# Attention with a mixture of adapters: results stored two chunks at a time, key rows loaded from another queue

## The chip, the cores and the metric

The kernel runs on one core of a Trainium2 chip. The core has five engines with a queue each, which run their instructions in the order written: TensorE (PE in the profile; its weight loads are PEld), VectorE (DVE), ScalarE (ACT), GpSimd (POOL) and SyncE (SP), which only issues transfers. Transfers (DMAs) are issued from SP, ACT and POOL and are carried by 16 DMA engines. The metric is the device time of one execution in microseconds (us); lower is better.

## The reference

```
kv_pool = kv.reshape(B, H//4, 4, W//4, 4, C).mean(axis=(2, 4))      # 4 x 384 x 32 -> 768 keys a batch
k = v = kv_pool.reshape(B, -1, C) @ w_sr
a = softmax(q @ k.T / sqrt(C));  x = a @ v                          # 4 x 12288 queries, C = 128
logits = x @ w_gate                                                 # 8 experts, the two best count
w = softmax over the two best logits
out = x + sum over the two of  w * ((x @ A[e]) @ B[e])              # rank 16
```

Inputs and the output are float32. The output has 49152 rows of 128 values, 25.2 MB.

## The kernel before, in words

The queries are cut into 96 chunks of 512; a batch has 24, and four chunks are a group. The work of a chunk is spread over several "slots" of a loop over k, one slot a chunk:

- Scores (`scores`, L307): PE multiplies the transposed queries `qT` by the keys `kfT` into the PSUM tile `sg`; ACT takes the exponential into `em`. Three such units make a chunk.
- Values (`attend`): PE multiplies `em` with `vx` into `acc`. `vx` has the values, the router's logits and a column of ones for the sum.
- Normalizing (`normalize`, L328 and L336): DVE divides into `xn`, which holds the attention's result and the logits.
- Routing (`top`, `route`, `gates`, L356 to L384): DVE finds the best logits, POOL and ACT make the gates `gw`.
- Adapters: `xn` is transposed, multiplied by all the A (`down`, tile `h_ps`), gated by DVE (`gate`, L437), transposed again, and multiplied by all the B (`up`, tile `d_ps`).
- The end of a chunk (`finish`, L471): DVE adds `d_ps` and `xn` into a result tile `osb`, and SP stores it (`store`, L467).

The second transpose is done in one of three ways. Chunks of the list `by_queue` (from 9 to 65, three of every four) go through a DMA transpose from SP (`gate_turn`, L457, tiles `ht` and `t`), and their `up` comes six or seven slots later. Chunks of `by_strip` (66 to 89) have both transposes done by DMA, in one transfer from SP a slot (`turn_dma`, L423, tile `turn`), read two or three slots later. The other chunks are transposed by PE (tile `tt_ps`).

Chunks are therefore not finished in the order of their numbers: an entry of `by_queue` comes several slots after its neighbour.

The queries of a group are cast by a DMA of POOL into bfloat16 in memory (`cast_q`, L83) and brought back by a DMA transpose of SP (`load_qT`, L92). Those of the first two groups are loaded in float32 (`load_q`) and transposed by PE.

The keys of a batch come from three tiles `kvr` of 2 MB; the pool has three of them. Each is loaded in four parts of 512 KB (`load_kv`, L102): the first batch and the second from SP, the third and the fourth from ACT, one part every two slots, at the start of the slot (`begin`). Parts of the last two batches are asked for from slot 15 to slot 37 and from 39 to 61. POOL sums the parts (`add_patches`, L522), five slots after a part is asked for and later, and PE transposes the sums.

The order of all the work is written out by hand: `keep` fixes it on each engine. Result tiles rotate: a new tile takes the buffer of the eighth before it (`opool`, eight buffers of 256 KB) and waits until that one's store has landed. In the list of instructions every DMA of SP and ACT also takes the next of eight completion semaphores, and waits for the DMA that had it before.

The four last chunks have code of their own (`carry`, `add_here`, `add_there`), with stores of 256 KB.

Of the kernel before, what the change touches and what calls it, by code (L numbers as in the profile page):

```python
# [10 lines left out]
FP32 = mybir.dt.float32  # L11
# [4 lines left out]
ALU = mybir.AluOpType  # L16
# [4 lines left out]
def kernel(  # L21
# [10 lines left out]
    nc = tc.nc  # L32
    P = 128
    B, N, C = q.tensor.shape
# [4 lines left out]
    T = 512  # L39
    S = T // P  # L40
    GC = 4
    GT = GC * T
# [4 lines left out]
    NCHUNK = B * NB  # L47
# [10 lines left out]
    gpool = ctx.enter_context(tc.tile_pool(name="gpool", bufs=6))  # L58
    run = ctx.enter_context(tc.tile_pool(name="run", bufs=3))
    hpool = ctx.enter_context(tc.tile_pool(name="hpool", bufs=4))  # L60
    opool = ctx.enter_context(tc.tile_pool(name="opool", bufs=8))
    qdram = ctx.enter_context(tc.tile_pool(name="qdram", bufs=1, space=bass.MemoryType.DRAM))
    ps_s = ctx.enter_context(tc.tile_pool(name="ps_s", bufs=2, space=bass.MemoryType.PSUM))
    ps_a = ctx.enter_context(tc.tile_pool(name="ps_a", bufs=1, space=bass.MemoryType.PSUM))
# [2 lines left out]
    keep = tc.keep_in_program_order  # L67
# [9 lines left out]
    q_bf, qT, kvr, spare = {}, {}, {}, {}  # L77
# [17 lines left out]
    def load_kv(b, h, r, x):  # L95

        if (b, h) not in kvr:
            kvr[b, h] = kvpool.tile([P, 4, 2, 4 * C], FP32, tag="kvr", name="kvr")
        rows = H // 3
        src = kv[b, h * rows + r:(h + 1) * rows:4].rearrange("y (w k) c -> y w (k c)", k=8)  # L100
        if x is None:
            keep((nc.scalar if b > 1 else nc.sync).dma_start(kvr[b, h][:, r].rearrange("p g c -> p (g c)"), src))  # L102
        else:
            keep(nc.sync.dma_start(kvr[b, h][:, r, x], src[:, :, x * 4 * C:(x + 1) * 4 * C]))


    q_f = {}

    def load_q(g, m):
        if g:  # L110
            t = hpool.tile([P, 2, S, P], BF16, tag="ht", name="qf")
            q_f[g, m] = t.rearrange("p h s c -> p (h s c)").bitcast(FP32).rearrange("p (s c) -> p s c", s=S)
        else:
            q_f[g, m] = opool.tile([P, S, C], FP32, tag="osb", name="qf")
        src = q[0, g * GT:(g + 1) * GT].rearrange("(p j) c -> p j c", p=P)
        keep(nc.sync.dma_start(q_f[g, m], src[:, m * S:(m + 1) * S]))

# [37 lines left out]
    def load_first(h):  # L155
        for r in range(3):
            load_kv(0, h, r, None)
        for x in range(2):
            load_kv(0, h, 3, x)

    load_first(0)
    for m in range(GC):
        load_q(0, m)
    load_first(1)
    load_first(2)
    for m in range(GC):
        load_q(1, m)
# [118 lines left out]
    em, acc, xn, xg, srt, gw = {}, {}, {}, {}, {}, {}  # L286
    used = []
    tts, xT, hgT, hp, hg, dp = {}, {}, {}, {}, {}, {}
# [53 lines left out]
    SOLO, TURN = NCHUNK - 6, NCHUNK - 28  # L342
# [122 lines left out]
    def store(queue, k, osb, lo=0, hi=S):  # L465
        to = out[k // GC * GT:(k // GC + 1) * GT].rearrange("(p j) c -> p j c", p=P)
        keep(queue.dma_start(to[:, k % GC * S + lo:k % GC * S + hi], osb))  # L467

    def finish(k):
        osb = opool.tile([P, S, C], FP32, tag="osb", name="osb")  # L470
        keep(nc.vector.tensor_tensor(osb, dp[k], xn[k][:, :, 0:C], op=ALU.add))  # L471
        store(nc.sync, k, osb)
        for d in (em, acc, xn, xT, hgT, hp, hg, dp):
            d.pop(k, None)

# [30 lines left out]
    for b in range(2, B):  # L506
        for n in range(12):
            h, r, t = n // 4, n % 4, b * NB - 33 + 2 * n
# [15 lines left out]
    def begin(k):  # L524
        nonlocal sums, rest
        b, i = divmod(k, NB)
        g = k // GC
        if k in casts:
            cast_q(4 + casts.index(k))
        if k in halves:  # L530
            g, u = halves[k]
            cast_q(g, u, u + 4)
        if k in rows_at:
            load_kv(*rows_at[k], None)
        if i == 0 and 0 < b < B - 1:
            rest = prepare(b + 1, nc.gpsimd)[1]
        if k == 3:
            sums, rest = prepare(1, nc.gpsimd)
            sums = sum(sums, [])
        if 3 <= k < 15:  # L540
            load_kv(1, (k - 3) // 4, (k - 3) % 4, None)
        if k == 7:
            for _ in range(2):
                sums.pop(0)()
# [12 lines left out]
    enter, t, left = {}, 1, list(range(NCHUNK - 3))  # L557
# [6 lines left out]
    by_queue = [k for k in range(9, TURN - 2) if k % 4 != 2 and k != 10]  # L564
    by_strip = range(TURN - 2, SOLO)
    slot = {x_: t for t, xs in enter.items() for x_ in xs}
    taken = [slot[x_] + (3 if x_ in by_strip else 2) for x_ in slot if x_ not in by_queue]
    up_slot = {}
    for x_ in by_queue:
        t = slot[x_] + (7 if x_ < TURN - 12 else 6)  # L570
# [2 lines left out]
        taken.append(t)  # L573
        up_slot[x_] = t
    by_pe = enter[SOLO - 2][1:]
    assert len(by_pe) == 1

    def up_at(k, x_):
# [46 lines left out]
    for k in range(k1, NCHUNK):  # L625
        b, i = divmod(k, NB)
        ka = att.get(k, [])
# [13 lines left out]
        if kx and not kd and all(x_ in by_dma for x_ in kx):  # L641
# [18 lines left out]
            for n in range(2):  # L660
                if n < len(ku):
                    up(ku[n])
                    finish(ku[n])
                attend(ka[0], n)
# [36 lines left out]
        for u_ in ku:  # L701
            up(u_)
            finish(u_)
# [17 lines left out]
        for x_ in kx[:1]:  # L721
            if x_ in by_queue:
                gate_turn(x_)
                up_at(up_slot[x_], x_)
                if k in loads:
                    load_qT(loads[k])
            elif x_ in by_strip:
                gate(x_, strip(k, 0)[:, 1])
                turn_dma(k, *todo, (hgT, x_))
                todo = []  # L730
                up_at(k + 3, x_)
            elif k == NCHUNK - 1:
                src, dst = (hpool.tile([P, 1, S, P], BF16, tag=tag, name=tag, bufs=3) for tag in ("h1", "t1"))
                gate(x_, src[:, 0])
                hgT[x_] = dst[:, 0]
                keep(nc.sync.dma_start(dst.rearrange("c h s p -> c (h s) p"),
                                       src.rearrange("p h s c -> p (h s c)"), transpose=True))
                up(x_ - 1)
                finish(x_ - 1)
            else:  # L740
                gate(x_)
# [86 lines left out]
        spread(dp[k, lo], lambda s: hgT[k][:, s], b_bf, lo, hi)  # L828

    def add_here(k, queue, lo=0, hi=S):  # L830
        osb = opool.tile([P, S, C], FP32, tag="osb", name="osb")[:, 0:hi - lo]
        keep(nc.vector.tensor_tensor(osb, dp[k, lo][:, lo:hi], xn[k][:, lo:hi, 0:C], op=ALU.add))
        store(queue, k, osb, lo, hi)

    def carry(k):
        osb = opool.tile([P, S, C], FP32, tag="osb", name="osb")
        keep(nc.scalar.copy(osb, dp[k, 0]))
        dp[k] = osb

# [35 lines left out]
    for s in range(S):  # L875
# [8 lines left out]
                                 op=ALU.is_ge))  # L884
# [3 lines left out]
    th = rpool.tile([P, S, E], FP32, tag="th1", name="th1")  # L888
    keep(nc.scalar.activation(th, arg, AF.Tanh, bias=0.0, scale=0.5))
    carry(K - 3)  # L890
    gw[K] = gpool.tile([P, S, E], FP32, tag="gw1", name="gw1")
    keep(nc.vector.scalar_tensor_tensor(gw[K], th, 1.0, mask, op0=ALU.add, op1=ALU.mult))
# [7 lines left out]
    fetch_h(K)  # L900
    up_into(K - 1, bank())
    add_here(K - 2, nc.sync)
    add_here(K - 1, nc.scalar)
    up_into(K, bank("s0"))
    add_here(K, nc.sync)


# [28 lines left out]
```

## Time and profile before

| what | value |
|---|---|
| three executions | 373.73, 373.82 and 378.04 us, median 373.82 |
| the profiled execution | 374.93 us, of which the span of the instructions is 372.8 |
| granted clock of PE | 0.996 |
| busy share of the span | PE 96%, PEld 75%, DVE 79%, ACT 79%, POOL 59% |
| moved | 88.09 MB in 75365 packets, mean 236 GB/s |
| stores of results | 95 of 256 KB from SP, median 4.8 us from issue to landing, and one from ACT |
| key rows | 24 loads of 512 KB from ACT (6.8 us), 21 of 512 KB and 6 of 256 KB from SP (7.3 and 7.7) |
| DMA transposes from SP | 22 of qT (8.6 us), 23 of turn (4.4), 16 of t (6.6), 14 of ht (5.9) |

How to read it: a busy share is a mean over the whole span, and engines run at the same time. A row of the timeline has the start (us from the start of the span), the length, the engine, the line, the operation with its tile and its inputs, the count, and in brackets how long the engine stood idle before and what ended that. "SPq" and "ACTq" are instructions of a queue that issue a transfer; their length is that of the issue, not of the transfer. A row of the waits has the engine and line that waited, what it waited for, the sum in us, the times and the longest. "kvr", "osb" and so on are the names of tiles.

### The profile page before, as it was taken

To read this page: it belongs to the slowest core of one execution; us is meant where nothing else is said; L and a number is where in the kernel's file an instruction comes from. 1 tells how busy PE (TensorE), PEld (TensorE's weight loads), DVE (VectorE), ACT (ScalarE), POOL (GpSimd) and SP (SyncE) were. 2 spreads that over 40 slices of the span, in tenths; PEclk is the share of its full clock that TensorE was granted. 3 is DMA by queue.
4 is the path that set the end of the run, shared out by engine and by line. 5 is a ranking of instruction groups with operands and counts; after the bars stand their busy time and mean duration, and the time that the engine had idled before them with its cause. 6 is when DMAs were issued, how large, how long until landed. Compare 5 with 4: busy or idle time off the path is not lost.

```text
span 372.8 us, 11165 instructions
## 1 busy us (share of the span) xinstructions
PE 358.9 (96%) x4262; PEld 281.2 (75%) x4268; DVE 292.8 (79%) x922; ACT 293.1 (79%) x364; POOL 218.6 (59%) x496
## 2 busy tenths in 40 slices
PE   7899999999999999899999999999999999999993
PEld 4577778877787787688787787787787777777782
DVE  1446789987888888688888888898897777778795
ACT  1448986878778886879878888888888999997873
POOL 1120368888766566566666756756757766665442
PEclk9999999999999999999999999999999999999998
DMA  7989659999989699999999999999899999999533
GB/s 248 380 295 227 228 163 288 306 262 269 242 242 225 205 171 290 253 308 263 280 229 260 272 233 255 197 259 186 222 210 199 269 231 226 225 228 205 158 101 141
DMA packets 75365, 88.09 MB, mean 236 GB/s; under 512 B 52048, under 2 KB 52304, under 8 KB 74960
## 3 DMA queue, kind: packets, MB, share of 16 engines
q1 hardware_dynamic: 68224, 62.93, 70.3%
q0 software_dynamic: 3200, 11.54, 17.6%
q10 hardware_dynamic: 3888, 12.92, 10.2%
q8 instruction: 33, 0.54, 0.6%
q14 instruction: 20, 0.16, 0.1%
HBM read 50.53 MB, written 36.70 MB: 234 GB/s over the span
## 4 chain that ended last, share of the span: by engine, by line
PE 84%; DMA 7%; DVE 3%; ACT 2%; POOL 1%; issue 1%; SPq 0%; ACTq 0%; DVEq 0%; POOLq 0%
PE acc L70 34%; PE sg L70 30%; PE tt_ps L70 5%; PE d_ps L70 5%; PE h_ps L70 5%; DMA kvr<-in_kv_dram 4%; PE kpT_ps L70 2%; DMA out_dram<-osb 2%; DMA turn<-turn 1%; ACT em L307 1%; PE v_ps L70 1%; DVE kvr L139 1%; DVE xn L336 1%; PE kfT_ps L70 1%; POOL kvr L225 1%
## 5 line engine op out<-in xcount | busy, mean ns | idle before, releaser
L307 ACT ACTIVATE em<-sg 128x1024 f16<-128x1024 f32 x288 | 283.3, 1022 | 60.8 <-PE sg L70 52.5
L70 PE MATMUL sg<-qT,kfT 128*128 128x512 bf16 x570 | 169.4, 379 | 2.9 <-ACT em L307 2.6
L70 PE MATMUL acc<-vx,em 128*128 128x136 f16 x2280 | 167.3, 223 | 0.1
L70 PEld LDWEIGHTS <-em 128*128 128x128 f16 x2304 | 146.8, 98 | 17.2 <-DVE xn L336 1.5
L336 DVE TENSOR_TENSOR xn<-acc,rinv 128x540 f32<-128x540 f32 x95 | 68.4, 720 | 3.3
L471 DVE TENSOR_TENSOR osb<-d_ps,xn 128x512 f32<-128x512 f32 x92 | 62.8, 688 | 2.0 <-PE d_ps L70 0.2
L368 POOL TENSOR_TENSOR over<-xn,srt 128x64 f32<-128x64 f32 (+1 forms) x120 | 31.0, 280 | 47.0 <-DVE srt L356 45.3
L522 POOL TENSOR_TENSOR kvr<-kvr 128x512 f32<-128x512 f32 (+1 forms) x48 | 57.0, 1204 | 0.5
L383 POOL TENSOR_TENSOR gw<-th,over 128x64 f32<-128x64 f32 (+1 forms) x60 | 17.4, 290 | 54.1 <-ACT th L381 53.8
L70 PEld LDWEIGHTS <-kfT 128*128 128x128 bf16 x576 | 45.2, 98 | 5.1 <-issue 3.1
L328 DVE RECIPROCAL rinv<-acc 128x4 f32<-128x4 f32 x95 | 17.3, 182 | 38.9 <-PE acc L70 36.0
L405 DVE COPY tts<-tt_ps 128x1024 bf16<-128x1024 bf16 (+1 forms) x73 | 36.8, 504 | 0.0
L70 PEld LDWEIGHTS <-xn 128*128 128x128 bf16 x296 | 22.5, 98 | 16.3
L356 DVE MAX8 srt<-xn 128x8 f32<-128x8 f32 x380 | 34.4, 152 | 0.1
L70 PEld LDWEIGHTS <-tts 128*128 128x128 bf16 x388 | 27.0, 98 | 7.0 <-DVE tts L405 0.4
L70 PE MATMUL h_ps<-a_bf,tts 128*128 128x128 bf16 x284 | 27.5, 219 | 0.0
L70 PE MATMUL tt_ps<-id_bf,xn 128*128 128x128 bf16 x284 | 27.4, 219 | 0.0
L374 POOL TENSOR_SCALAR over<-over 128x64 f32<-128x64 f32 (+1 forms) x60 | 19.9, 332 | 5.3
L437 DVE TENSOR_TENSOR hg<-h_ps,gw 128x512 bf16<-128x512 f32 x26 | 17.9, 688 | 6.1 <-POOL gw L384 5.3
L437 DVE TENSOR_TENSOR hs<-h_ps,gw 128x512 bf16<-128x512 f32 x28 | 19.1, 683 | 4.3 <-POOL gw L384 3.9
L227 POOL TENSOR_TENSOR kvr<-kvr 128x512 f32<-128x512 f32 x18 | 22.5, 1272 | 0.0
L70 PEld LDWEIGHTS <-turn 128*128 128x128 bf16 x180 | 13.6, 98 | 10.4 <-issue 0.9
(97 smaller groups left out, 301.4 us busy)
## 6 DMA issues: line engine op xcount, KB each, us to landing
out_dram<-osb SPq DMA_DIRECT2D x95, 256.0 KB, 4.8
kvr<-in_kv_dram ACTq DMA_DIRECT2D x24, 512.0 KB, 6.8
kvr<-in_kv_dram SPq DMA_DIRECT2D x21, 512.0 KB, 7.3
qbf<-in_q_dram POOLq DMA_DIRECT2D x20, 512.0 KB, 8.3
qf<-in_q_dram SPq DMA_DIRECT2D x8, 256.0 KB, 7.6
kvr<-in_kv_dram SPq DMA_DIRECT2D x6, 256.0 KB, 7.7
qbf<-in_q_dram POOLq DMA_DIRECT2D x4, 256.0 KB, 5.4
turn<-turn SPq DMA_TRANSPOSE x23, 4.4
```

Source lines behind the costliest of these rows:

```text
L70: return keep(nc.tensor.matmul(*a, **k))
L227: keep(adder.tensor_tensor(u[:, lo:hi], u[:, lo:hi], v[:, lo:hi], op=ALU.add))
L307: keep(nc.scalar.activation(o, i_, AF.Exp, bias=0.0, scale=scale))
L336: keep(nc.vector.tensor_tensor(x[:, :, 0:VC], acc[k][:, :, 0:VC], ri.unsqueeze(2).broadcast_to([P, S, VC]), op=ALU.mult))
L356: keep(nc.vector.max(srt[k0][:, m, s], xn[k][:, s, C:C + E]))
L368: keep(eng.tensor_tensor(d, lg, so[:, :, i].unsqueeze(2).broadcast_to([P, n, 8]), op=ALU.subtract))
L374: keep(eng.tensor_scalar(mask, mask, 0.0, None, op0=ALU.is_ge))
L383: keep(eng.tensor_tensor(w[:, 0:n], th, mask, op=ALU.mult))
L405: keep(nc.vector.tensor_copy(sb[:, lo:hi], ps[:, lo:hi]))
L437: keep(nc.vector.tensor_tensor(hg[k].rearrange("p s (e r) -> p (s e) r", e=E), hp[k].rearrange("p s (e r) -> p (s e) r", e=E), gw[k0][:, m ...
L471: keep(nc.vector.tensor_tensor(osb, dp[k], xn[k][:, :, 0:C], op=ALU.add))
L522: keep(nc.gpsimd.tensor_tensor(u, u, v, op=ALU.add))
```

## The change

`finish` now works in pairs. A list `done` is made beforehand that has the chunks 0 to 91 in the order in which they are finished; two that follow each other there share one result tile of 512 KB. DVE writes the half of the chunk with the lower number or that with the higher one, and the second of the two to be finished issues one DMA for both. Where the two chunks are neighbours in a group this DMA writes 4 KB runs (14 of 46 in the list of instructions), otherwise 2 KB runs in two places. `opool` has four buffers of 512 KB instead of eight of 256 KB. The first group's queries, which use the same pool before any result is there, are loaded into the halves of such tiles, and the last four chunks use half of one.

`load_kv` now issues every load of key rows from SP, at the same place of the loop.

```diff
-    opool = ctx.enter_context(tc.tile_pool(name="opool", bufs=8))
+    opool = ctx.enter_context(tc.tile_pool(name="opool", bufs=4))
...
-            keep((nc.scalar if b > 1 else nc.sync).dma_start(kvr[b, h][:, r].rearrange("p g c -> p (g c)"), src))
+            keep(nc.sync.dma_start(kvr[b, h][:, r].rearrange("p g c -> p (g c)"), src))
...
-            q_f[g, m] = opool.tile([P, S, C], FP32, tag="osb", name="qf")
+            if m % 2 == 0:
+                q_f[g, "t"] = opool.tile([P, 2, S, C], FP32, tag="osb", name="qf")
+            q_f[g, m] = q_f[g, "t"][:, m % 2]
...
+    mate = []
+
     def finish(k):
-        osb = opool.tile([P, S, C], FP32, tag="osb", name="osb")
-        keep(nc.vector.tensor_tensor(osb, dp[k], xn[k][:, :, 0:C], op=ALU.add))
-        store(nc.sync, k, osb)
+        n = done.index(k)
+        ka, kb = sorted(done[n - n % 2:n - n % 2 + 2])
+        if n % 2 == 0:
+            mate[:] = [opool.tile([P, 2, S, C], FP32, tag="osb", name="osb")]
+        osb = mate[0]
+        keep(nc.vector.tensor_tensor(osb[:, int(k == kb)], dp[k], xn[k][:, :, 0:C], op=ALU.add))
+        if n % 2:
+            at = [k_ // GC * GT * C + k_ % GC * T // P * C for k_ in (ka, kb)]
+            to = bass.AP(tensor=out.tensor, offset=out.offset + at[0],
+                         ap=[[GC * S * C, P], [at[1] - at[0], 2], [1, S * C]])
+            keep(nc.sync.dma_start(to, osb.rearrange("p i s c -> p i (s c)")))
...
+    done = [1, 0]
+    for t in range(8, NCHUNK):
+        done += [x_ for x_ in slot if x_ not in by_queue and (x_ not in by_strip or x_ in by_pe) and slot[x_] + 2 == t
+                 and x_ > 1]
+        done += [x_ for x_ in slot if x_ not in done and
+                 (up_slot.get(x_) == t or x_ in by_strip and slot[x_] + (3 if slot[x_] < SOLO - 3 else 2) == t)]
+    done.append(NCHUNK - 5)
...
     def add_here(k, queue, lo=0, hi=S):
-        osb = opool.tile([P, S, C], FP32, tag="osb", name="osb")[:, 0:hi - lo]
+        osb = opool.tile([P, 2, S, C], FP32, tag="osb", name="osb")[:, 0, 0:hi - lo]
```

More of the change, by code (lines that the diff above doesn't have):

```diff
@@ L575 @@
     by_pe = enter[SOLO - 2][1:]
+    done = [1, 0]
[5 more added lines that the diff above has]
+    done.append(NCHUNK - 5)
+    assert sorted(done) == list(range(NCHUNK - 4)), done
     assert len(by_pe) == 1
@@ L835, in carry @@
     def carry(k):
-        osb = opool.tile([P, S, C], FP32, tag="osb", name="osb")
+        osb = opool.tile([P, 2, S, C], FP32, tag="osb", name="osb")[:, 0]
         keep(nc.scalar.copy(osb, dp[k, 0]))
```

## The prediction

> **What bounds the kernel now.** I read the page's first part, then the busy time by stretches, to see where the bounding engine ever stops; then the timeline at the stops.
>
> ```profile
> span 372.8 us, 11165 instructions
> PE 358.9 (96%) x4262; PEld 281.2 (75%) x4268; DVE 292.8 (79%) x922; ACT 293.1 (79%) x364; POOL 218.6 (59%) x496
> PE 84%; DMA 7%; DVE 3%; ACT 2%; POOL 1%; issue 1%; SPq 0%; ACTq 0%; DVEq 0%; POOLq 0%
> 75.00:148.00 73.00, 72.81 (x890) 57.38 (x888) 61.44 (x195) 58.95 (x70) 52.07 (x92) 1.00 1.05 239
> 150.00:275.00 125.00, 124.40 (x1538) 98.80 (x1537) 105.61 (x329) 104.16 (x125) 77.56 (x149) 1.00 1.08 248
> 275.00:345.00 70.00, 69.52 (x835) 53.76 (x834) 54.66 (x179) 63.08 (x85) 46.78 (x153) 1.00 1.08 221
> ```
>
> The last three rows are stretches of the steady part: after the length, busy time of PE, PEld, DVE, ACT and POOL, the granted clock, the DMA share and GB/s. TensorE (PE) works 72.81 of 73, 124.40 of 125 and 69.52 of 70 us at a clock of 1.00; it is the bound, and in these 268 us it misses 1.27 us. The DMA engines are as full (1.05 to 1.08), but the chain that ended last is PE for 84%: transfers are issued early enough to hide. The one real stop lies in the two microseconds that I left out:
>
> ```profile
> 141.08 1.48 SPq L467 DMA_DIRECT2D out_dram<-osb  x3
> 148.54 4.19 SPq L92 DMA_TRANSPOSE qT<-qbf  x1
> 148.83 0.59 ACTq L102 DMA_DIRECT2D kvr<-in_kv_dram  x1
> 149.52 2.85 ACT L307 ACTIVATE em<-sg 128x1024 f16<-128x1024 f32 x3 [2.77 <-DMA out_dram<-osb]
> 150.60 0.59 PE L70 MATMUL sg<-qT,kfT 128*128 128x512 bf16 x2 [1.88 <-ACT em L307]
> ```
>
> ScalarE (ACT) runs its queue in order, and here it holds a load of key rows (L102) at the head: the load leaves at 148.83, when a store issued on SyncE (SP) at 141.08 lands. In the instruction list the DMAs of both queues take turns on eight completion semaphores, and each waits for the eighth before it. The exponentials (L307) behind the load wait 2.77 us, and PE, which needs their score banks back, 1.88 us. That stop is the change's to win.
>
> **The key rows: 24 loads leave ACT for SP.** Normally the load costs ACT nothing:
>
> ```profile
> 138.05 1.02 ACT L307 ACTIVATE em<-sg 128x1024 f16<-128x1024 f32 x1
> 138.82 0.54 ACTq L102 DMA_DIRECT2D kvr<-in_kv_dram  x1
> 138.95 1.03 ACT L307 ACTIVATE em<-sg 128x1024 f16<-128x1024 f32 x1
> L102 ACTq DMA_DIRECT2D kvr<-in_kv_dram x24: 542/542/620, 74.4 to 240.0; - x24
> L102 SPq DMA_DIRECT2D kvr<-in_kv_dram x21: 534/576/1358, 0.7 to 71.9; - x21
> ```
>
> The issue takes 0.54 us of the sequencer, but the next exponential starts 0.90 us after the one before, its usual step: 24 x 0.54 = 13.0 us are hidden behind the running activation. What goes is the waiting: I take -1.9 us, bounded by 0 (a run in which no load of the 24 is held) and by -1.9 - 1.27 = -3.2 us (every stop of the steady part).
>
> On SP the loads stand behind stores and transposes. Who waits for them is GpSimd (POOL), which adds the rows in order ahead of the routing gates:
>
> ```profile
> 239.95 0.54 ACTq L102 DMA_DIRECT2D kvr<-in_kv_dram  x1
> 261.53 2.49 POOL L522 TENSOR_TENSOR kvr<-kvr 128x512 f32<-128x512 f32 x2
> 115.67 8.64 SPq L92 DMA_TRANSPOSE qT<-qbf  x1
> 133.06 7.93 SPq L92 DMA_TRANSPOSE qT<-qbf  x1
> kvr<-in_kv_dram ACTq DMA_DIRECT2D x24, 512.0 KB, 6.8
> kvr<-in_kv_dram SPq DMA_DIRECT2D x21, 512.0 KB, 7.3
> DMA to landing us min/median/max: 4.1/7.1/10.4
> ```
>
> The last of the 24 is issued at 239.95 and its rows are first added at 261.53: 21.6 us, of which the longest landing of key rows takes 10.4 (the last row is that of tile kvr) and the longest hold of SP by one transpose 8.64. 21.6 - 10.4 - 8.64 leaves 2.6 us: no cost; without this cover a late load costs PE what POOL waits.
>
> The Trainium skill ("DMA: Bandwidth & Descriptors", Queues, rings and completion order) has a rule against this move: SP and ACT each own a ring on each of the 16 engines, which serve the rings in turn, so on SP the rows lose their own share and queue behind the transposes. The trace has 7.3 us from SP and 6.8 from ACT, so the rule would cost half a microsecond of hidden latency here.
>
> **The stores: 92 of 256 KB become 46 of 512 KB.** Issue time on SP, from these rows:
>
> ```profile
> L467 SPq DMA_DIRECT2D out_dram<-osb x95: 332/402/1331, 48.8 to 369.1; - x95
> SPq L467 <- DVE srt L356: 54.2, 33, 8.9
> out_dram<-osb SPq DMA_DIRECT2D x95, 256.0 KB, 4.8
> ```
>
> Away go 92 x 0.40 = 37.0 us. A 512 KB store isn't in the trace; its issue is bounded by 0.40 us (one store) and 0.80 (two), and I take the 0.58 of a 512 KB load on SP: 46 x 0.58 = 26.5, plus 24 x 0.58 = 13.8 for the loads, 40.3 in all. SP gains 3.3 us of issuing over the whole run and had 54.2 us of idle waiting for VectorE (DVE) in front of stores alone: nothing on the path. In the instruction list 14 pairs are neighbours (4 KB runs), the other 32 stay 2 KB runs, so the bytes are moved as before. Fewer DMAs also make "the eighth before" older: per four chunks nine become seven.
>
> The result buffer is four of twice the size instead of eight. DVE fills the first half, and the pair's store goes with the second; the buffer is needed again seven results later, some 7 x 3.4 = 24 us (320.3 us between the first and the last of the 95 stores above, over 94), against 10.4 at most to land:
>
> ```profile
> DMA to landing us min/median/max: 2.0/4.8/10.4
> ```
>
> That row is the stores'. Cost 0. In the instruction list, in the steady part, every other pair store also waits for the pair store before it, as their address ranges interleave; the earlier one has had two chunks' time, 6.8 us, by then. Between a landing of 4.8 and one of 10.4 that holds SP for 0 to 3.6 us, out of its 54.2 idle ones: 0 again. The opening keeps its order on PE, and the last four stores their size.
>
> What isn't hidden by much are the transposes of the late chunks (L423, tile turn), read by PE two chunks later:
>
> ```profile
> 302.17 2.70 SPq L92 DMA_TRANSPOSE qT<-qbf  x1
> 304.96 0.53 SPq L467 DMA_DIRECT2D out_dram<-osb  x1
> 305.60 1.31 SPq L423 DMA_TRANSPOSE turn<-turn  x1
> 300.70 0.23 PEld L70 LDWEIGHTS <-turn 128*128 128x128 bf16 x4 [0.59 <-DMA turn<-turn]
> 310.14 0.27 PEld L70 LDWEIGHTS <-turn 128*128 128x128 bf16 x4 [0.27 <-DMA turn<-turn]
> PEld L70 <- DMA turn<-turn: 0.9, 2, 0.6
> turn<-turn SPq DMA_TRANSPOSE x23, 4.4
> GB/s 248 380 295 227 228 163 288 306 262 269 242 242 225 205 171 290 253 308 263 280 229 260 272 233 255 197 259 186 222 210 199 269 231 226 225 228 205 158 101 141
> ```
>
> PE waits twice for one (0.59 and 0.27 us), each right after a q transpose and a store. At 300.70 there were two 256 KB stores ahead, now one of 512 KB: equal. At 310.14 there was one, now one twice as large. The extra 256 KB take 0.7 us at the best rate of the GB/s row (380) and 1.1 at its 236 mean; bounds are 0, if the store has drained, and 2.5 us (7.3 of a 512 KB load less 4.8 of a store). I take the middle of the rates, +0.9; the others have the odd store taken from in front of them as often as enlarged.
>
> **Sum.** The profiled execution took 374.93 us (span 372.8): 374.93 - 1.9 + 0.9 = 373.9. It stands 1.1 above the median of the runs, 373.82. If the median run has the whole stop, it comes to 373.82 - 1.0 = 372.8; if the 1.1 is part of the stop, 0.8 is left to win and it stays at 373.82 - 0.8 + 0.9 = 373.9. I take 373.4. Two per cent, about what a measurement of this kernel can tell from no change, are 366.3 and 381.3.
>
> **The rivals.**
> - Late turns (slower). If every one of the 23 transposes comes 0.6 us late, as the worse of the two does, PE waits 13.8 us instead of 0.9: 373.4 - 0.9 + 12.9 = 385.4. It decides where the landing passes some 5.2 us:
>
> ```profile
> 295.43 1.79 SPq L423 DMA_TRANSPOSE turn<-turn  x1
> 295.43 5.23 DMA turn<-turn
> ```
>
> That one (second row: its piece of the chain) was the one waited for at 300.70. For it: median 4.4, and DMA engines that are full. Against it: the bytes stay, and half the turns lose their store.
> - Late key rows (slower). If a load is held by two q transposes in a row, 8.64 + 7.93 + 10.4 - 21.6 = 5.4 us late, POOL stops, then the gates, then PE; at two such places +10.8: 384.2. For it: the two long transposes are neighbours. Against: seven DMAs per four chunks instead of nine on the eight semaphores, and two loads between the transposes.
> - It does not do what it says: no load is held in most runs, or SP's hold moves to another wait, and only the turn is left: 373.82 + 0.9 = 374.7. For it: the stop comes once in 24 loads.
> - ACT's issues were on the path after all (faster): 373.4 - 13.0 = 360.4. Against it: the 0.90 us step above, and the 1.27 us that PE idles; even with the stop that is 3.2 us, under 1%.
>
> **How the numbers follow.** Forecast 0.70, no gain 0.15, late turns 0.07, late key rows 0.05, ACT 0.03. Faster by over 2% is the last, 0.03; slower the two late ones, 0.12; within 0.85. The forecast's own range is 371.5 to 375.6: 372.8 less the 1.27, and 374.7 with one more turn 0.9 late. The whole range goes from 370.5 (372.8 - 0.9 - 1.27, no turn late) to 380.0 (a little over half of the late turns, 373.4 + 6.0), and leaves out the full rivals.
>
> **What would show it.** Right: no exponential ended by a DMA, PE over 99% in the stretches around 150, two or three waits for turn under 1.8 us in all, 46 stores with 0.5 to 0.8 us of issue. Wrong: a wait of POOL L522 for key rows, of DVE's result for a store, more than five waits for turn, or a PE that idles over 3 us between 75 and 345.

## The result, and the profile after

| | before | after |
|---|---|---|
| executions beside each other, 22 each | median 373.74, from 372.34 to 378.04 us | median 378.70, from 373.53 to 393.69 us |
| executions above 378 us | 1 of 22 | 15 of 22 |
| profiled execution (span) | 374.93 (372.8) | 381.86 (380.1) |

The ratio of after to before is 1.0065, 95% interval 1.0036 to 1.0095: slower, by less than 2%. The ratio leaves out executions more than 1.5% above the fastest of their kernel, which are ten of the 22 of after and one of before, so the counts above 378 us say more than it does. The fastest execution of after (373.53) is about as fast as the median of before (373.74); what the change brought is that most executions fall behind somewhere. The profiled one is of that kind, so a second profile of the same kernel, of an execution of 376.95 us (span 375.1), stands beside it below.

From the page of after, the rows that answer to those shown of before, and the waits of PE and POOL for transfers:

```profile
span 380.1 us, 11047 instructions
PE 361.2 (95%) x4262; PEld 281.4 (74%) x4268; DVE 293.2 (77%) x922; ACT 293.9 (77%) x364; POOL 218.7 (58%) x496
PE 73%; DMA 18%; DVE 3%; ACT 1%; POOL 1%; issue 1%; SPq 1%; DVEq 0%; ACTq 0%; POOLq 0%
out_dram<-osb SPq DMA_DIRECT2D x46, 512.0 KB, 6.3
kvr<-in_kv_dram SPq DMA_DIRECT2D x45, 512.0 KB, 6.9
PE sg L70 <- DMA qT<-qbf: 3.2, 2, 2.5
PE h_ps L70 <- DMA turn<-turn: 2.4, 3, 1.8
PE d_ps L70 <- DMA ht<-hs: 1.2, 1, 1.2
POOL kvr L534 <- DMA kvr<-in_kv_dram: 3.4, 2, 2.9
```

The span is 7.3 us longer: 5.0 us in which PE does nothing (380.1 - 361.2 against 372.8 - 358.9), and 2.3 us more of busy PE for the same 4262 matmuls. In the chain DMA has gone from 7% to 18%. The stop of ACT is gone: no wait of ACT for a DMA is left. New are waits of PE for q transposes (`qT`), which had none before. By stretches of 50 us (length, busy time of PE, PEld, DVE, ACT and POOL with counts, clock, DMA share, GB/s), before, then after, then the second profile of after:

```profile
125.00:175.00 50.00, 48.12 (x592) 38.04 (x589) 41.28 (x130) 39.09 (x47) 30.32 (x58) 1.00 1.09 264
175.00:225.00 50.00, 50.00 (x623) 39.77 (x621) 43.14 (x136) 41.35 (x50) 31.61 (x60) 1.00 1.04 258
275.00:325.00 50.00, 49.86 (x595) 38.38 (x594) 38.80 (x131) 45.50 (x61) 34.57 (x112) 1.00 1.09 221
```

```profile
125.00:175.00 50.00, 49.28 (x606) 38.77 (x604) 42.54 (x134) 40.03 (x48) 30.32 (x58) 1.00 1.11 207
175.00:225.00 50.00, 46.35 (x550) 36.22 (x549) 37.77 (x120) 37.58 (x45) 29.55 (x57) 0.97 1.05 247
275.00:325.00 50.00, 47.57 (x567) 36.35 (x566) 37.44 (x122) 42.89 (x56) 31.41 (x101) 1.00 1.11 217
```

```profile
125.00:175.00 50.00, 48.90 (x599) 38.30 (x597) 41.95 (x133) 40.19 (x48) 30.23 (x60) 1.00 1.09 206
175.00:225.00 50.00, 48.10 (x598) 38.13 (x597) 41.13 (x128) 39.61 (x47) 30.78 (x59) 1.00 1.07 275
275.00:325.00 50.00, 48.74 (x583) 37.47 (x581) 37.54 (x125) 44.59 (x60) 32.99 (x108) 1.00 1.11 229
```

Both profiles of after lose in the same two places. In the stretch from 125 the transfers move 207 and 206 GB/s where before moved 264, with the DMA engines as busy (1.11, 1.09, 1.09; the share adds up the times of all packets, so above 1 some of them overlap); PE pays for it up to 225 (4.37 and 3.00 us idle in the 100 us, against 1.88 before, all of that the stop of ACT). From 275 on, where the `turn` transposes begin, PE idles 2.43 and 1.26 us against 0.14. SP's queue shows what goes ahead of the stops in the first place (timeline of after; the second number is how long the issue held the queue):

```profile
127.84 1.07 SPq L102 DMA_DIRECT2D kvr<-in_kv_dram  x1
129.00 0.59 SPq L484 DMA_DIRECT2D out_dram<-osb  x1
129.65 1.35 SPq L459 DMA_TRANSPOSE t<-h  x1
131.09 13.26 SPq L92 DMA_TRANSPOSE qT<-qbf  x1
...
186.66 8.55 SPq L92 DMA_TRANSPOSE qT<-qbf  x1
198.59 1.03 PE L70 MATMUL sg<-qT,kfT 128*128 128x512 bf16 x2 [2.45 <-DMA qT<-qbf]
```

A q transpose that is issued behind key rows, a pair's store and a small transpose holds SP for 13.26 us; in the profile of before the longest hold was 8.64. The next two q transposes are issued at 152.46 and 172.38, where before they were at 148.54 and 160.70; for the third, of 186.66, PE stands for 2.45 us. The largest stop for a `turn`:

```profile
295.42 3.24 SPq L92 DMA_TRANSPOSE qT<-qbf  x1
298.72 0.58 SPq L484 DMA_DIRECT2D out_dram<-osb  x1
299.46 1.81 SPq L425 DMA_TRANSPOSE turn<-turn  x1
307.64 0.23 PEld L70 LDWEIGHTS <-turn 128*128 128x128 bf16 x4 [2.26 <-DMA turn<-turn]
```

The transpose issued at 299.46, behind a q transpose and a 512 KB store, is read at 307.64, 8.2 us later, where before the one read late took 5.23.

### The profile page after: what moved, and what is told of

Its sections match the earlier page's. It is cut to its first block, busy times and chain, and to the rows that moved or that the text cites. A ratio compares the mean times of both kernels' runs of the same rounds, so it can differ in the third digit from the quotient of the medians.

```text
span 380.1 us, 11047 instructions
## 1 busy us (share of the span) xinstructions
PE 361.2 (95%) x4262; PEld 281.4 (74%) x4268; DVE 293.2 (77%) x922; ACT 293.9 (77%) x364; POOL 218.7 (58%) x496
## 4 chain that ended last, share of the span: by engine, by line
PE 73%; DMA 18%; DVE 3%; ACT 1%; POOL 1%; issue 1%; SPq 1%; DVEq 0%; ACTq 0%; POOLq 0%
PE acc L70 30%; PE sg L70 27%; DMA qT<-qbf 7%; DMA kvr<-in_kv_dram 6%; DMA turn<-turn 6%; PE tt_ps L70 5%; PE h_ps L70 5%; PE d_ps L70 5%; ACT em L309 1%; PE v_ps L70 1%; PE kpT_ps L70 1%; DVE xn L338 1%; POOL kvr L227 1%; DVE tts L407 0%; DVE hg L867 0%
```

## The experiments

Four accounts were set against each other. A: key rows in SP's queue do the harm, standing between transposes. B: the 512 KB stores do, as bursts ahead of transposes. C: with fewer, larger DMAs on eight semaphores more bytes stand ahead of a transpose. D, from the fifth kernel on: the DMA engines have almost no time to spare, so that a delay, whatever caused it, isn't made up. The measure is the count of executions above 378 us, a line drawn once the first result was known; before had 4 such in 101 (1 of 22, 0 of 11, 3 of 23, 0 of 11 and 0 of 34 on five occasions).

### Each part alone

Pairs alone (after, with the key rows back on ACT), and the repeat:

```diff
-            keep(nc.sync.dma_start(kvr[b, h][:, r]...
+            keep((nc.scalar if b > 1 else nc.sync).dma_start(kvr[b, h][:, r]...
```

> The changed kernel with the key rows of the last two batches back on ScalarE; results still stored two chunks at a time. Theory A (the key rows in SyncE's queue do the harm: there they stand in line with the q transposes, whose issue grew from at most 8.6 to 13.3 us): as fast as before or better, 371 to 374 us in nearly every execution, q transposes issued in at most 9 us, no wait of PE for qT or ht. Theory B (the 512 KB stores do the harm, as bursts in the ring ahead of the transposes): spread and slow as the changed kernel, 374 to 390 us, with waits of PE for qT, ht and turn.

> A repeat of the pairs alone (key rows of batches 2 and 3 stay with ScalarE), with more executions beside those of before. If the pairs alone bring the spread: 4 to 6 in 11 executions above 377, against 1 in 11 of before. If the spread needs both parts: 1 or 2 in 11. The fastest ones at 373 in both cases.

Measured: medians 378.39 and 378.09, fastest 373.06, 3 of 6 and 3 of 6 above 378; ratios 1.0013 (0.9959 to 1.0068) and 1.0027 (0.9978 to 1.0076). Key rows alone (before, with all key rows on SP), and the repeat:

```diff
-            keep((nc.scalar if b > 1 else nc.sync).dma_start(kvr[b, h][:, r]...
+            keep(nc.sync.dma_start(kvr[b, h][:, r]...
```

> The kernel before with only the key rows moved from ScalarE to SyncE; stores of 256 KB as before. Theory A: spread upwards, 374 to 390 us, and with nine transfers in four chunks on one queue rather worse than the changed kernel. Theory B: 371 to 374 us, without the stop of ScalarE behind a held load.

> A repeat of the key rows on SyncE alone (stores of 256 KB, one per chunk), with more executions. If the key rows alone bring the spread (A): 4 to 6 in 11 executions above 377, against 1 in 11 of before. If it needs both parts: 1 or 2 in 11. The fastest ones at 372.5 to 373 in both cases.

Measured: medians 374.96 and 373.31, fastest 372.54, 2 of 6 and 2 of 6 above 378; ratios 0.9982 (0.9937 to 1.0027) and 0.9977 (0.9936 to 1.0018). So each part alone brings long executions, in 6 of 12 and 4 of 12, beside none of 22 of before, and neither ratio differs from 1 by more than its interval. The profiles tell the two places apart. Pairs alone (the execution of 375.89), then key rows alone (379.68):

```profile
125.00:175.00 50.00, 50.00 (x621) 39.84 (x620) 43.20 (x136) 41.28 (x49) 31.87 (x62) 1.00 1.07 257
175.00:225.00 50.00, 50.00 (x624) 39.89 (x622) 43.28 (x136) 41.39 (x49) 31.64 (x61) 1.00 1.14 254
275.00:325.00 50.00, 47.85 (x552) 36.53 (x549) 35.30 (x117) 42.74 (x57) 31.34 (x102) 0.97 1.06 211
```

```profile
125.00:175.00 50.00, 48.15 (x591) 37.88 (x590) 41.36 (x130) 40.49 (x49) 30.77 (x60) 1.00 1.14 213
275.00:325.00 50.00, 45.80 (x550) 35.23 (x549) 35.45 (x118) 41.79 (x56) 31.43 (x102) 1.00 1.08 213
```

The loss between 125 and 225, with its 206 to 213 GB/s, is in both profiles of after and in both of the key rows alone (208 GB/s in the other one); it is in neither of the pairs alone (257 and 263). The loss after 275 is in all of them. In the other profile of key rows alone the latter is one stop:

```profile
280.36 4.88 SPq L92 DMA_TRANSPOSE qT<-qbf  x1
285.97 1.30 SPq L423 DMA_TRANSPOSE turn<-turn  x1
290.02 0.61 PE L70 MATMUL h_ps<-a_bf,turn 128*128 128x128 bf16 x4 [4.97 <-DMA turn<-turn]
```

The first `turn` is issued at 285.97; in before it was at 277.39, as SP wasn't behind when the late chunks began. For the first place this fits A; the second comes without key rows on SP too.

### The key rows on a third queue

With pairs (after, `nc.gpsimd` for the last two batches in place of `nc.sync`), and with single stores (before, `nc.gpsimd` in place of `nc.scalar`), two times each:

> The changed kernel with the key rows of the last two batches issued by GpSimd. Theory A in its form 'SyncE's queue': a third queue of its own is as good as ScalarE's and holds no exponential: 371 to 374 us. If instead it is the absence of ScalarE's ring as such, or any tighter packing of the DMA engines, it is spread like the changed kernel, 375 to 385 us. GpSimd pays some 0.6 us for each of the 24 issues, ahead of the gates, which it has to spare (59% busy).

> A repeat of pairs with the key rows of batches 2 and 3 on GpSimd. If the pairs are safe as long as SyncE's and ScalarE's queues carry no key rows: none or one in six above 378. If it was luck and any edit of the order brings the spread: two to four in six.

> The kernel before, with one edit: the key rows of batches 2 and 3 are loaded by GpSimd; stores stay 256 KB, one per chunk. ScalarE loses its stops (1.9 us in the chain of before), SyncE's queue stays as it is. A (key rows in SyncE's queue do the harm): 1 to 2 us faster than before, 372.5, with few executions above 378. DMA capacity (the bytes of the steady part nearly fill the 16 DMA engines, and any delay lasts): the bytes are those of before and the order is nearly that of before, so 373 to 374.5, with one execution in ten above 378, like before. Were both wrong and the stop of ScalarE what keeps the transfers apart, then above 376 with half the executions above 378.

> A repeat of single stores with the key rows on GpSimd. With the run before (4 of 6 above 378): again three or more of six, if this order really tips over more often than that of before; none or one, if it was luck.

Measured with pairs: medians 373.18 (ratio 0.9967, 0.9935 to 0.9999) and 374.37 (0.9991, 0.9958 to 1.0024), 4 of 18 above 378. With single stores: 380.43 and 375.74 (ratios 1.0018, 0.9958 to 1.0079, and 1.0001, 0.9968 to 1.0034), 8 of 18 above 378, although no queue of SP or ACT was lengthened and the stores are those of before. That speaks against A and B as whole explanations, and my own forecast by D (one in ten) was a miss as well. It is the third case of that forecast, the stop of ACT keeping the transfers apart, that came nearest: half of the executions above 378 (the medians, 380.43 and 375.74, lie on both sides of its 376). The long hold isn't special to key rows on SP either: in the first run with single stores (the execution of 385.20 us) q transposes hold SP for 12.91 us at 186.17 and for 12.10 at 210.59, the rate from 175 to 225 is 198 GB/s, and PE then waits 4.7 us for one; with pairs alone one holds it for 12.27. The gain of the first run with pairs didn't come back in the second.

The Trainium skill ("DMA: Bandwidth & Descriptors", Issuing engines are not separate DMA queues) says that issuing from several engines saves only issue time, since all transfers run on the same 16 DMA engines. That agrees with this: a third queue for 12.6 MB of key rows took neither the waits nor the long executions away.

### Two small stores at the pair's place

```diff
-            keep(nc.sync.dma_start(to, osb.rearrange("p i s c -> p i (s c)")))
+            for i in range(2):
+                store(nc.sync, (ka, kb)[i], osb[:, i])
```

> The changed kernel, but each pair's result is stored by two transfers of 256 KB, issued one behind the other where the pair's was. The same bytes stand at the same places of SyncE's queue; there are nine transfers in four chunks again instead of seven, so the eighth before is nearer, and no store waits for another's address range. Theory C (the fewer, larger transfers let more bytes stand ahead of a transpose): executions above 378 us become rare, 372 to 375. Theory B (bulk that isn't urgent stands in the queue in bursts ahead of transposes that are): no change, about half above 378 us.

Measured: median 375.33, ratio 1.0013 (0.9975 to 1.0052), 5 of 12 above 378. As many DMAs as before and none of 512 KB among the stores, and still the long executions: neither the size of one DMA nor a smaller number of them (C) is needed. B as bursts, two stores in a row ahead of a transpose, had forecast this (about half above 378) and isn't touched by it; against B stand the key rows alone and the key rows on POOL with single stores, whose stores are those of before. In the profile of this run (378.46) nothing is lost before 225, at 258 GB/s from 125 on with the key rows on SP, and 4.16 us from 275 to 325: key rows on SP don't bring the first place every time.

### Fewer bytes, more bytes

After, with only one half of each pair's results stored (46 of 92 left out), and with one half of every second pair's (23 left out):

```diff
-            keep(nc.sync.dma_start(to, osb.rearrange("p i s c -> p i (s c)")))
+            store(nc.sync, ka, osb[:, 0])                # every pair; or, if n % 4 == 1, every second one
```

> The changed kernel, with only one half of each pair stored (256 KB instead of 512; the result of the other chunk is left out): same count and order of transfers, 12 MB of 88 fewer. If the cause is that the DMA engines have too little time to spare (theory A and B alike): 371 to 373 us in every execution, no wait for qT, q transposes issued in under 8 us. If it is the order and the waits of SyncE's queue alone, whatever the bytes: still spread to 380 us and more.

> The kernel after, with one edit: of every second pair only the first chunk's result is stored, as 256 KB (23 of 92 results are left out, 6 MB of 88). DMA capacity: half the dose of the run with 12 MB less takes most of the spread away: median 372.5 to 374, one execution in ten above 378. Places in the queue or burst sizes (A, B): 23 of the pairs and all key rows stand where they stood in after, so the spread stays: a median of 376 or more, with at least 4 in 11 above 378.

Measured: 372.28 (ratio 0.9951, 0.9928 to 0.9975), all 12 executions between 371.98 and 373.51; and 371.90 (0.9936, 0.9905 to 0.9967), all 11 between 371.51 and 373.86, as D had it. The other direction is before, with the result of every second chunk stored once more, into scratch memory:

```diff
         store(nc.sync, k, osb)
+        if k % 2 == 0:
+            again = qdram.tile([P, S * C], FP32, tag=f"again{k}", name=f"again{k}")
+            keep(nc.sync.dma_start(again, osb.rearrange("p s c -> p (s c)")))
```

> The kernel before, with one edit: of every second chunk the result is stored a second time, into scratch DRAM (22 or 23 more stores of 256 KB, 6 MB on 88), from SyncE. DMA capacity: at a little less than full, 6 MB more push the steady part over it, so a median of 378 to 390 and most executions above 378, with waits of PE for qT, ht and turn. A and B (places in the queue, 512 KB bursts): the stores are of the size of before and an issue costs SyncE 0.58 us, 13 of 54 idle us, so within 2 us of before, 374 to 376, few above 378.

Measured: 401.04, all six between 391.17 and 417.02. The edit had twice the dose that I wrote, 46 stores and 12 MB, and the time went past the 378 to 390 that I had written. This run isn't a clean test of the bytes: the 46 stores also lengthen SP's queue and the turns of the eight semaphores, and in its profile ACT stands once for 8.5 us behind a load that is held for one of them. The DMA queues' rows (packets, MB, and the time that the packets took, as a share of the 16 engines' span) of before, of after, of after with 12 MB less and with 6 MB less, and of before with 12 MB more:

```profile
q1 hardware_dynamic: 68224, 62.93, 70.3%
q0 software_dynamic: 3200, 11.54, 17.6%
q10 hardware_dynamic: 3888, 12.92, 10.2%
```

```profile
q1 hardware_dynamic: 69152, 75.51, 79.5%
q0 software_dynamic: 3200, 11.54, 18.4%
q10 hardware_dynamic: 432, 0.33, 0.3%
```

```profile
q1 hardware_dynamic: 65056, 63.46, 70.9%
q0 software_dynamic: 3200, 11.54, 18.4%
```

```profile
q1 hardware_dynamic: 67104, 69.48, 76.0%
q0 software_dynamic: 3200, 11.54, 18.9%
```

```profile
q1 hardware_dynamic: 74848, 74.99, 73.6%
q0 software_dynamic: 3200, 11.54, 17.3%
q10 hardware_dynamic: 3888, 12.92, 9.6%
```

With q8 (0.6% in each) and q10 (0.3%) added where they aren't shown, the packets' time is 98.7% of the engines' span in before and 98.8% in after, 90.2% with 12 MB less, 95.8% with 6 MB less, and 101.1% with 12 MB more; as packets can overlap, this tells how crowded the engines are and isn't a hard limit. With 6 or 12 MB less the same places in the same queues, key rows on SP and 23 pairs included, bring no long execution: 0 of 23 above 378, against 21 of 34 of after. With 12 MB more the order of before fails too. The share doesn't tell a long execution from a short one of the same bytes: it is 98.4% with pairs and key rows on POOL at 372.45 us, and 97.8% with key rows alone at 383.07. In the profile with 6 MB less the q transposes of the first place hold SP shorter, and the rate is back (window from 125; and the q transposes under way between 120 and 225, shortest, median and longest hold in ns, with 6 MB less, then after). A later one of that profile (last row of the first block) holds SP longer than any in after:

```profile
125.00:175.00 50.00, 50.00 (x621) 39.75 (x619) 43.03 (x136) 41.26 (x49) 31.66 (x62) 1.00 1.07 251
L92 SPq DMA_TRANSPOSE qT<-qbf x8: 3017/5600/8024, 115.6 to 218.2; - x8
230.35 14.98 SPq L92 DMA_TRANSPOSE qT<-qbf  x1
```

```profile
L92 SPq DMA_TRANSPOSE qT<-qbf x7: 3960/8134/13264, 116.1 to 215.0; - x7
```

PE waits 0.2 us in all for q transposes in that execution: a long hold isn't enough for a loss, and here it was caught up. So the runs with fewer bytes show D's main point: with the places unchanged, the long executions depend on the bytes. Whether it is the time of the DMA engines or the writes to memory that have too little room isn't separated, since both fall together. What is left at 6 MB less are short stops: 1.98 us from 275 to 325 in this profile, of an execution of 373.81 us.

### Two tries to mend it

All bulk transfers off SP: key rows of the last batches, and pairs from the seventh on, issued by POOL (`nc.gpsimd if n > 12 else nc.sync`).

> The changed kernel with the key rows of the last two batches and nearly all pair stores issued by GpSimd, so that SyncE has the transposes nearly alone. If what hurts is that bulk stands ahead of the transposes in one queue: the transposes land sooner (turn under 4 us, q transposes under 8), few waits for them, 371 to 374 us. If the total load of the DMA engines decides whatever the queue: spread as the changed kernel. A risk of its own: GpSimd's queue waits for DVE's results and for the landing of the store before, and the gates behind it come late; then it is slower by 5 us or more with waits for gw.

Measured: 392.06, ratio 1.0461 (1.0406 to 1.0515). POOL's queue is also that of the routing gates, and it now waits for the stores' places:

```profile
DVE hs L439 <- POOL gw L386: 14.7, 14, 4.9
POOL out_dram L484 <- DMA out_dram<-osb: 7.2, 2, 5.0
```

The q transposes asked for two slots earlier, from group 9 to 19 (`4 * g - 8` for `4 * g - 6`):

> The changed kernel with the q transposes of groups 9 to 19 issued two chunks (some 7 us) earlier. If PE loses its time because these land too late: slack for qT grows by 7 us, the waits for qT go, and most executions are at 372 to 376 us; waits for ht and turn may stay. If qT is only one of several that are late together: no better than the changed kernel, 376 to 390 us.

Measured: 385.10, ratio 1.0243 (1.0184 to 1.0302). PE's waits for `qT` are gone, and as large ones have come for the next transfers on SP:

```profile
PEld L70 <- DMA turn<-turn: 6.9, 3, 5.5
PE h_ps L70 <- DMA turn<-turn: 5.3, 2, 5.0
```

### After once more

> The kernel after, unchanged, beside the others on the same chip: 3 or 4 of 6 above 378, if the spread belongs to the kernel and not to the chip that it first ran on.

Measured: median 377.57, from 372.99 to 391.31, 6 of 12 above 378, beside none of 34 of before on that chip (ratio 1.0018, 0.9971 to 1.0065). The long executions belong to the kernel; this is also the execution of 376.95 us above. The interval holds 1 this time, so the ratio of 1.0065 wasn't repeated; the long executions were. In all, 21 of 34 of after are above 378.

## Why the prediction was wrong

- **The bound and its cover.** That PE bounds was right. "The DMA engines are as full (1.05 to 1.08), but ... transfers are issued early enough to hide" is the root of the miss: I took a full set of DMA engines for harmless because the waits were few. In after a lateness often wasn't made up; with six MB less, 7% of the bytes, it was, and every execution lies within 371.51 to 373.86. PE idles 7.3 us between 75 and 345 in the one profile of after and 4.8 in the other, over the 3 us that I had named as a sign of being wrong.
- **ACT's stop, -1.9.** Right: no exponential is ended by a DMA in either profile of after. In the profiles of pairs alone PE works 50.00 of 50 us twice from 125 on, against 48.12.
- **The key rows, "21.6 - 10.4 - 8.64 leaves 2.6 us: no cost".** This is the step that failed. It took the longest hold of SP by a q transpose, 8.64 us, over from one profile of before; in after it was 13.26 us (13.17 in the second profile, 13.21 and 13.31 with the key rows alone), and 21.6 - 10.4 - 13.26 is 2.1 us too late. What lengthens a hold isn't shown: holds of 12 to 13 us also came with pairs alone and with the key rows on POOL. The step also asked only whether POOL gets its rows in time. POOL did wait (3.4 us in 2 waits, which I had named as a sign), but PE's price was paid at transfers that I had not costed, the q transposes themselves (3.2 us in 2 waits) and `ht` (1.2).
- **The rule that I set aside.** I quoted the Trainium skill ("DMA: Bandwidth & Descriptors", Queues, rings and completion order), by which rows on SP lose the share of their own that ACT's ring gave them, and priced it at half a microsecond by the landing times. The rows themselves indeed landed in 6.9 us; the transposes behind them are what became late. The rule was to be weighed for what stands behind the moved DMA too. The lost share isn't the whole cause: on POOL the rows have a queue of their own (q0 in the profile), and 12 of 36 executions were long.
- **The stores' issue.** Sized right (0.54 us each where I took 0.58; 6.3 us to land, below the 7.3 of the bound). "Nothing on the path" is the second term put at nothing that failed: pairs alone have 6 long executions of 12, with stops of PE for `turn`.
- **Buffer of four pairs, cost 0.** Right: no result of DVE waits for a store.
- **The turn, +0.9, bounds 0 to 2.5.** The right place, sized too small: in the row that I used (PEld's waits for `turn`) 0.9 us became 3.9 in the one profile and 2.2 in the other, +3.0 and +1.3; PE itself idles 2.4 us in 3 waits and 1.2 in 2. As a rival it was given every one of 23 turns 0.6 us late; what came is a few, each up to 2.3, and one of 5.0 in the key rows alone, where SP starts the late chunks behind.
- **The sum, 373.4 against 378.70.** The range (370.5 to 380.0; its lower end adds up to 370.6) holds it, and the change is within 2%, as was likeliest; but I forecast a small gain and got a loss, with the whole interval of the ratio above 1 in the 22 executions each and a median 1.0% up in the repeat. The sum was made for one execution as if it were all: nothing in it could give a median 1.3% up with the fastest up by only 0.3% (373.53 against 372.34).
- **What stays open.** Why the order of before has 4 long executions in 101 and six other orders of the same bytes between 4 of 18 and 21 of 34 isn't settled (the two tries to mend it, also of the same bytes, have 12 of 12). Nor is it known whether a long execution of before looks like one of after, as none was profiled. That ACT's hold of a load keeps the transfers of before apart would fit (pairs alone have neither the hold nor the calm), but no run separates it from the order of the DMAs; it is argued only. What makes one execution fall behind and the next not, with the same program, isn't seen either.

## What to carry to other kernels

Look at the share of the DMA engines' time that packets take before moving a transfer. Here, at 98.7%, none of the new places for stores and key rows was free: price a moved DMA by everything that stands behind it too, and count how often an execution falls behind, since the cost shows there more than in the fastest one. Taking some bytes away in an experiment, with every place kept, shows whether room for the transfers is what lacks; here 7% less was enough. And compare distributions, not one profile: a profile of pairs alone at 373.06 us would have passed for a gain.

## What was not expected of the hardware

The time that a DMA transpose holds its issuing queue isn't a property of the transpose: the 22 `qT` transfers of an execution held SP for 1.8 to 8.6 us in before and for 2.6 to 13.3 in after; for 2.3 to 6.8 with 12 MB less, but for 2.5 to 15.0 with 6 MB less, and for 2.4 to 16.0 with 12 MB more. What sets it isn't shown; the amount of bytes alone doesn't.

A long stop of PE can cost more than its length. The clock granted was lower for a while after one (after, in stretches of 10 us):

```profile
190.00:200.00 10.00, 7.55 (x87) 5.81 (x85) 6.32 (x20) 4.27 (x5) 3.75 (x6) 0.93 1.00 258
200.00:210.00 10.00, 10.00 (x115) 7.80 (x113) 7.34 (x25) 8.11 (x11) 5.81 (x12) 0.90 1.02 243
210.00:220.00 10.00, 10.00 (x126) 7.82 (x123) 8.75 (x28) 8.58 (x11) 6.63 (x12) 1.00 1.27 327
```

After the stops of 1.2 and 2.45 us between 189 and 199 PE gets 0.93 and then 0.90 of its clock, and does 115 matmuls in 10 us where it later does 126. The missing 0.07 and 0.10 of 10 us are 1.7 of the 2.3 us of longer busy time, beside the 5.0 us of idling. After the shorter stops, 1.88 us in before and 1.72 in the second profile of after, the rows of 10 us stay at 1.00; in the stretch of 50 us from 275 with the stop of 4.97 (key rows alone) the clock is 0.93.
